# Batch 0's heads 0 to 3 loaded and attended ahead of heads 4 to 7, in a retention layer fused with a feed-forward layer

## The chip, the cores and the metric

The kernel runs on one core of a Trainium2 chip. A core has TensorE (matrix products and transposes, results into PSUM), VectorE, ScalarE and GpSimd (elementwise work), and SyncE, whose queue issues nearly all transfers here. PSUM has eight banks that the kernel shares out by tags. The metric is device time of one execution in microseconds (us). The kernel before takes 296.96 us, the median of three runs (296.57 to 297.06).

## The reference

Eight batches, eight heads, 576 positions, 64 numbers per head. Scores are masked and damped by a power of the distance, not normalised, and the result goes through a layer with a swish of a learned slope.

```python
scores = scale * np.matmul(q, k.transpose(0, 1, 3, 2))
gamma = 1.0 - 2.0 ** (-5.0 - np.arange(H))
rel = pos[:, None] - pos[None, :]
Dmat = np.where(rel >= 0, gamma[:, None, None] ** rel[None], 0.0)
attn = np.matmul(scores * Dmat, v)                 # (8, 8, 576, 64)
x = attn.transpose(0, 2, 1, 3).reshape(4608, 512)
h = x @ w_in                                       # 512 -> 2048
out = (h / (1.0 + np.exp(-beta * h))) @ w_out      # 2048 -> 512
```

## The kernel before

A power of a distance splits into two factors: queries are multiplied by `gamma**pos` (`gq`, with the scale in it), and either keys or values by `gamma**-pos` (`gvh` for batch 0, `gv` later). What is left of the damping is a mask of ones and zeros. Because nothing is normalised, earlier positions can be gathered in a state, the sum of key times value: a block's output is its own masked scores times values ("O") plus its queries times the state of all blocks before it ("cross").

The first 512 positions of each batch are attended in blocks, and batches follow one another; the last 64 positions of all batches make one more block of work. For each batch the outputs are laid down turned (`xT`), and the feed-forward layer runs on them: the up-projection `ph` (16 groups `fo` of 128 columns, each four products over `ko`, the four groups of 128 rows of `w_in`), a Silu on ScalarE into `gT`, and the down-projection `po` (16 products for each of four row groups `ms`). `ko` 0 and 1 need heads 0 to 3 alone, `ko` 2 and 3 heads 4 to 7. All is cast to bf16 before TensorE uses it. The order of all instructions is written out by hand (`manual_schedule`): each engine has one queue that it works in program order, and waits on semaphores of the others. `merged` weaves the lists `streams` into the list `fill`: an entry `(x, f)` is emitted before the fill item with the next number.

The change is in the first stage, batch 0, which nothing precedes. Its 512 positions are cut into two spans of 256 (`s` = 0, 1), and its heads into two halves (`a` = 0 for heads 0 to 3, 1 for 4 to 7). The steps, as functions:

- `load_q` (L75) and `load_span` (L99): SyncE issues the loads of queries (a half, 512 KB) and of keys or values (`j` = 0, 1; a span and half, 256 KB).
- `pre_q` (L282): VectorE scales queries, two operations for each half. `t_q` (L348): TensorE turns them, eight transposes for a half, and one copy brings them into `qT`; ScalarE copies for half 0, VectorE for half 1.
- `pre_s` (L456): GpSimd casts or scales keys or values. Half 0 casts its keys and scales its values, half 1 scales its keys and casts its values.
- `s_T` (L469): four transposes of keys, and ScalarE's copy into `kT`. `s_sc` (L483): sixteen score products, and two masks on VectorE into `R`.
- `s_O` (L497): sixteen products of values and masked scores. `s_st` (L519): products for the state, up to three block borders in PSUM tiles `s_sts`. `s_keep` (L530): two copies of a state into its tile `sbds`, on the engines that are passed in. `s_cross` (L508): queries times the state. `s_x` (L515): the copy into `xT`.
- `keep_warm` (L246): a product of the identity with itself, 512 columns, whose result nobody reads. The text calls it a filler.
- `betas`, `betas_safe` (L251, L256): the slopes are turned, and three small GpSimd operations keep them from being zero.

These are called one after the other on lines 726 to 780, and then the feed-forward layer begins: `cast_w_in` (L209) casts pieces of `w_in`, which SyncE loads ahead of all else behind the spans, as 256 or 512 columns of two or four row groups (`pieces`, L193). `ups` (L661) is an up-projection of several `fo` in two steps, `u` = 0 for `ko` 0 and 1 and `u` = 1 for 2 and 3; `up` (L648) does all four. `rest` (L782) has what of the attention is not needed for the first step: the crosses and `xT` of half 1. `last_products` and `last_state` make the state of the whole batch, for the last 64 positions. `down` (L681) splits the products of batch 0 from `fo` 5 on into two of 256 columns. The casts of `w_out` follow its loads.

## Time and profile before

| | us |
|---|---|
| median of three runs | 296.96 |
| the profiled execution's own time | 297.28 |
| its span | 295.5 |
| TensorE busy | 287.1 (97%) |
| ScalarE, GpSimd, VectorE busy | 145.9, 111.1, 102.5 |
| 5.79 to 16.66, attention of batch 0: span, TensorE busy | 10.87, 10.35 |
| 16.66 to 31.64, up-projection of batch 0: span, TensorE busy | 14.98, 14.86 |

Each instruction has a start and a duration; products are pipelined, so that the distance between starts, not the duration, is what a product costs in a stream. "Idle before" an instruction is put down to what released it. The chain of waits goes back from the last instruction to what released it. The profiled execution is one run; its own time is 1.8 us above its span and 0.32 above the median. Landings of loads are read from the semaphores of the transfers: low queries 4.93, high queries 6.42, keys and values from 7.32 to 13.61, pieces of `w_in` from 14.37 to 26.20.

### The profile page before, as it was taken

The numbers are of one execution on the slowest core, as the hardware profiler recorded it, in microseconds if no ns is written. First come the engines' busy times: TensorE is split into PE (matmuls) and PEld (weight loads), VectorE is DVE, ScalarE is ACT, GpSimd is POOL, SyncE is SP. The second block draws the span as 40 slices with busy tenths as digits, with TensorE's granted clock in tenths as the row PEclk, the third lists the DMA queues.
The fourth block names the chain that finished last, engine by engine and source line by source line (L and its number), as shares of the span: only waits on it lengthen the run. The fifth ranks groups of instructions, "written<-read, shape, count | busy, mean of one in ns | idle before, by whom it ended". The sixth has DMA issues, their size and how long they took to land.

```text
span 295.5 us, 7656 instructions
## 1 busy us (share of the span) xinstructions
PE 287.1 (97%) x3245; PEld 150.6 (51%) x3274; DVE 102.5 (35%) x213; ACT 145.9 (49%) x255; POOL 111.1 (38%) x219
## 2 busy tenths in 40 slices
PE   7999999999999999999999999999999999999995
PEld 3654587855544554445444544454554544444443
DVE  5764546604640551045204530354053500110012
ACT  5657537783278434843474347434780167007600
POOL 5957027955733713280438316754223000000000
PEclk9999999999999999999999999999999999999999
DMA  7999999999999898949999849998998110131011
GB/s 225 306 367 386 376 226 277 220 180 253 222 229 235 214 162 231 252 72 161 231 250 198 180 105 273 190 177 180 219 174 138 73 38 0 35 71 38 0 71 71
DMA packets 124033, 53.97 MB, mean 183 GB/s; under 512 B 101840, under 2 KB 116448, under 8 KB 124000
## 3 DMA queue, kind: packets, MB, share of 16 engines
q1 hardware_dynamic: 123968, 53.49, 82.1%
q8 instruction: 25, 0.41, 0.6%
q14 instruction: 8, 0.07, 0.1%
q10 hardware_dynamic: 32, 0.01, 0.0%
HBM read 36.71 MB, written 9.44 MB: 156 GB/s over the span
## 4 chain that ended last, share of the span: by engine, by line
PE 96%; DMA 1%; issue 1%; ACT 0%; DVE 0%; DVEq 0%
PE po L690 42%; PE ph L655 38%; PE ph L670 4%; PE O L614 2%; PE sc L568 1%; PE st L586 1%; DMA qn<-in_q_dram 1%; PE O L627 1%; PE T L352 1%; PE st L527 1%; PE sc L378 0%; PE sc L490 0%; PE O L504 0%; ACT kT L475 0%; PE ph L248 0%
## 5 line engine op out<-in xcount | busy, mean ns | idle before, releaser
L690 PE MATMUL po<-w_out_sb,gT 128*128 128x512 bf16 (+3 forms) x619 | 125.7, 358 | 2.3 <-issue 2.1
L657 ACT ACTIVATE gT<-ph,beta_sb 128x512 bf16<-128x512 f32 (+1 forms) x140 | 91.5, 659 | 50.9 <-PE ph L655 50.5
L655 PE MATMUL ph<-xT,w_in_sb 128*128 128x512 bf16 (+1 forms) x550 | 114.4, 364 | 0.5
L690 PEld LDWEIGHTS <-gT 128*128 128x128 bf16 x636 | 60.2, 98 | 60.7
L655 PEld LDWEIGHTS <-w_in_sb 128*128 128x128 bf16 x560 | 54.3, 98 | 57.5 <-DVE first L594 0.4
L697 DVE COPY ot<-po 128x512 f32<-128x512 f32 (+2 forms) x33 | 22.2, 672 | 72.2 <-PE po L690 69.4
L328 POOL CAST kn<-kvn 128x128 bf16<-128x128 f32 (+2 forms) x76 | 23.4, 343 | 46.1 <-DMA kvn<-in_k_dram 41.2
L295 POOL TENSOR_TENSOR qs<-qn,gq 128x256 bf16<-128x256 f32 (+1 forms) x36 | 26.3, 756 | 33.1 <-DMA qn<-in_q_dram 33.1
L575 DVE TENSOR_TENSOR R<-sc,tri 128x512 bf16<-128x512 f32 x28 | 17.4, 684 | 60.0 <-PE sc L568 60.0
L306 POOL TENSOR_TENSOR vn<-kvn,gv 128x512 bf16<-128x512 f32 x28 | 29.1, 1040 | 7.4 <-DMA kvn<-in_v_dram 7.1
L642 ACT CAST xT<-O 128x512 bf16<-128x512 f32 x14 | 7.5, 590 | 31.6 <-PE O L627 31.6
L597 ACT CAST sbd<-warm 128x256 bf16<-128x256 f32 x18 | 7.3, 407 | 25.6 <-DVE warm L594 20.6
L670 PE MATMUL ph<-xT,w_in_sb 128*128 128x512 bf16 x54 | 12.8, 379 | 0.1
L594 DVE TENSOR_TENSOR first<-st,warm 128x256 f32<-128x256 f32 x24 | 10.2, 425 | 2.9 <-ACT sbq L597 0.5
L316 POOL TENSOR_TENSOR kn<-tln,gq 128x128 bf16<-128x128 f32 (+1 forms) x12 | 5.6, 470 | 14.2 <-DMA tln<-in_q_dram 9.9
L594 DVE TENSOR_TENSOR warm<-st,first 128x256 f32<-128x256 f32 x18 | 7.6, 423 | 9.6 <-PE st L586 8.4
L673 ACT ACTIVATE gT<-ph,beta_sb 128x512 bf16<-128x512 f32 x14 | 8.7, 688 | 4.4 <-PE ph L670 4.4
L642 DVE CAST xT<-O 128x512 bf16<-128x512 f32 x14 | 9.0, 686 | 5.1 <-PE O L627 5.1
L214 POOL CAST w_in_sb<-wt 128x256 bf16<-128x256 f32 (+1 forms) x15 | 7.7, 530 | 5.0 <-DMA wt<-in_moe_w_in_dram 4.9
L597 ACT CAST sbd<-first 128x256 bf16<-128x256 f32 x18 | 7.3, 407 | 2.2 <-DVE first L594 0.2
L670 PEld LDWEIGHTS <-w_in_sb 128*128 128x128 bf16 x56 | 5.2, 97 | 6.3 <-issue 0.5
L231 DVE TENSOR_SCALAR w_out_sb<-wt,rbeta_sb 128x512 bf16<-128x512 f32 x13 | 5.9, 485 | 5.0 <-DMA wt<-in_moe_w_out_dram 5.0
(107 smaller groups left out, 166.1 us busy)
## 6 DMA issues: line engine op xcount, KB each, us to landing
qn<-in_q_dram SPq DMA_DIRECT2D x16, 512.0 KB, 5.2
kvn<-in_k_dram SPq DMA_DIRECT2D x32, 256.0 KB, 6.1
kvn<-in_v_dram SPq DMA_DIRECT2D x32, 256.0 KB, 5.1
out_dram<-ot SPq DMA_DIRECT2D x31, 256.0 KB, 3.4
wt<-in_moe_w_out_dram SPq DMA_DIRECT2D x8, 512.0 KB, 8.5
wt<-in_moe_w_in_dram SPq DMA_DIRECT2D x5, 512.0 KB, 8.8
wt<-in_moe_w_in_dram SPq DMA_DIRECT2D x6, 256.0 KB, 5.6
tln<-in_q_dram SPq DMA_DIRECT2D x8, 128.0 KB, 3.6
```

The costliest lines, as they stand in the source:

```text
L295: nc.gpsimd.tensor_tensor(batch[b]["qs"][:, cs, to], q_tiles[b][:, hs, cs].rearrange("p h i d -> p i h d"), gq[:, cs, hs].unsqueeze(3).to_ ...
L306: nc.gpsimd.tensor_tensor(live[i]["vn"], kv_tiles.pop(i)[:, 1], gains(gv, c), ALU.mult)
L328: nc.gpsimd.tensor_copy(kn[:, c % 2, to], t[:, 0, hs])
L575: nc.vector.tensor_tensor(R[x][:, j].rearrange("k c p q -> k (c p) q"), sc[x, j].rearrange("k c p q -> k (c p) q"), mask, ALU.mult)
L594: nc.vector.tensor_tensor(new[:], add, sums[(c - 1) % 2][:], ALU.add)
L597: nc.scalar.copy((sbq[c] if c < NC - 1 else ends[u])[:], new[:])
L642: (nc.scalar.copy if n % 2 else nc.vector.tensor_copy)(x, o)
L655: nc.tensor.matmul(ph, w_in_sb[:, ko, fo * P:(fo + 1) * P], xts[m][:, ko, :, w], start=(ko == 0), stop=(ko == KO - 1))
L657: nc.scalar.activation(gts[m][:, fo, :, w], ph, ACT.Silu, scale=beta_sb[:, fo:fo + 1])
L670: nc.tensor.matmul(phs[f][:], w_in_sb[:, ko, f * P:(f + 1) * P], xts[m][:, ko], start=(ko == 0), stop=(ko == KO - 1))
L690: nc.tensor.matmul(po[:, x:y], gT[:, fo, ms, :], w_out_sb[:, fo, n0 + x:n0 + y], start=(fo == 0), stop=(fo == FO - 1), skip_group_check=m ...
L697: (nc.scalar.copy if m == 0 else nc.vector.tensor_copy)(ot, po[:, :nn])
```

## The change

The loads of batch 0 come in another order: queries of heads 0 to 3, their keys, queries of heads 4 to 7, keys of span 0, values of heads 0 to 3, keys of span 1, values of heads 4 to 7. All keys are now cast and all values scaled. The turned queries of heads 4 to 7 are copied by ScalarE instead of VectorE in batch 0; two of the four copies of turned keys go to VectorE (`s_T` gets the engine and the bank passed in). The calls in the prelude are put in another order, with nine fillers in place of five, and `betas_safe` behind the first two key casts. The states are numbered by block, use other PSUM tiles, and the second span's are copied by ScalarE (two) and VectorE (one). `w_in`'s fourth piece is loaded in two transfers; `fo` 4 to 7 go through `ups`, the banks of the up-projection's results change, the last state products come one fill item earlier, and down-projections of batch 0 are split from `fo` 7 on.

```diff
--- before.py
+++ after.py
@@ -122,10 +122,11 @@
             for x in range(2):
                 nc.sync.dma_start(to[x * TL:(x + 1) * TL], src[2 * t + x, :, MB:, :].rearrange("h s d -> s h d"))
 
-    load_q(0)
-    span_order = [(s, j, a) for j in range(2) for a in range(2) for s in range(2)]
-    for x in span_order:
+    load_q(0, (0,))
+    for n, x in enumerate([(0, 0, 0), (1, 0, 0), (0, 0, 1), (0, 1, 0), (1, 1, 0), (1, 0, 1), (0, 1, 1), (1, 1, 1)]):
         load_span(*x)
+        if n == 1:
+            load_q(0, (1,))
     beta_rows = consts.tile([FO, P], F32, name="beta_rows")
     nc.scalar.dma_start(beta_rows[:], moe_beta.rearrange("(fo p) -> fo p", p=P))
 
@@ -190,7 +191,7 @@
     WG = 4
 
     low_rows, high_rows = slice(0, KO // 2), slice(KO // 2, KO)
-    pieces = [(f, 256, (low_rows, high_rows) if f < 768 else (slice(0, KO),)) for f in range(0, d_ff // 2, 256)]
+    pieces = [(f, 256, (low_rows, high_rows)) for f in range(0, d_ff // 2, 256)]
     pieces += [(f, 512, (w,)) for f in range(d_ff // 2, d_ff, 512) for w in (low_rows, high_rows)]
     NP = len(pieces)
     w_in_r = moe_w_in.rearrange("(ko ki) f -> ki ko f", ki=P)
@@ -243,10 +244,11 @@
             nc.tensor.matmul(ph[:, :cols], warm[:, :P], src, start=True, stop=True,
                              skip_group_check=True)
 
-    def keep_warm(tag="mm"):
+    def keep_warm(n=1, tag="mm"):
         ph = psum.tile([P, CB, P], F32, name="ph", tag=tag, bufs=3 if tag == "mm" else 1)
-        nc.tensor.matmul(ph[:], ident[:], ident[:].unsqueeze(1).to_broadcast([P, CB, P]), start=True, stop=True,
-                         skip_group_check=True)
+        for _ in range(n):
+            nc.tensor.matmul(ph[:], ident[:], ident[:].unsqueeze(1).to_broadcast([P, CB, P]), start=True, stop=True,
+                             skip_group_check=True)
 
     def betas():
         pb = psum.tile([P, FO], F32, name="pb", tag="mm", bufs=3)
@@ -350,7 +352,7 @@
         for i in range(CB):
             for p in range(2):
                 nc.tensor.transpose(T[:, i, p, :], heads(batch[b]["qs"][:, i], 2 * u + p), ident[:])
-        (nc.vector.tensor_copy if u else nc.scalar.copy)(batch[b]["qT"][:, :, 2 * u:2 * u + 2], T[:])
+        (nc.vector.tensor_copy if b and u else nc.scalar.copy)(batch[b]["qT"][:, :, 2 * u:2 * u + 2], T[:])
 
     def t_k(i):
         T = psum.tile([P, HP, P], BF16, name="T", tag="sc" if i in (CB + 2, CB + 3) else "O", bufs=2)
@@ -461,18 +463,18 @@
                             kT=sb.tile([P, 2, HP, P], BF16, name="kT", tag="kT", bufs=4),
                             vn=sb.tile([P, 2, H, D], BF16, name="vn", tag="vn", bufs=VB), R={})
         to, src = spans[s]["kv"[j] + "n"][:, :, w], span_tiles[s, j][:, w].rearrange("p h i d -> p i h d")
-        if a == j:
+        if j == 0:
             nc.gpsimd.tensor_copy(to, src)
         else:
             nc.gpsimd.tensor_tensor(to, src, gvh[:, 2 * s:2 * s + 2, w].unsqueeze(3).to_broadcast([P, 2, HP, D]), ALU.mult)
 
-    def s_T(s, a):
+    def s_T(s, a, tag, e):
         S = spans[s]
-        T = psum.tile([P, 2, 2, P], BF16, name="T", tag="O", bufs=2)
+        T = psum.tile([P, 2, 2, P], BF16, name="T", tag=tag, bufs=3 if tag == "mm" else 2)
         for i in range(2):
             for pl in range(2):
                 nc.tensor.transpose(T[:, i, pl, :], heads(S["kn"][:, i], 2 * a + pl), ident[:])
-        act(S["kT"][:, :, 2 * a:2 * a + 2], T[:])
+        e(S["kT"][:, :, 2 * a:2 * a + 2], T[:])
 
     def s_q(c, r, p):
         return batch[0]["qT"][r, :, p, c * PC:(c + 1) * PC]
@@ -519,7 +521,7 @@
     def s_st(a, n, s, rows, at=None, fresh=False):
 
         if n not in s_sts:
-            s_sts[n] = psum.tile([P, HP, P], F32, name="st", tag="mm" if n else "st", bufs=3 if n else 1)
+            s_sts[n] = psum.tile([P, 2 if n == 3 else HP, P], F32, name="st", tag="st" if n == 1 else "mm", bufs=1 if n == 1 else 3)
             fresh = True
         S, at = spans[s], 2 * a if at is None else at
         for i in range(2):
@@ -527,13 +529,13 @@
                 nc.tensor.matmul(s_sts[n][:, at + p, :], heads(S["kn"][rows, i], 2 * a + p), heads(S["vn"][rows, i], 2 * a + p),
                                  start=fresh and i == 0 and p == 0, stop=True, skip_group_check=True)
 
-    def s_keep(a, n, es, bank=None, at=None):
+    def s_keep(a, c, es, n=None, at=None):
 
         ps, at = slice(2 * a, 2 * a + 2), 2 * a if at is None else at
         for j in range(2):
-            st = s_sts[min(n, 1) if bank is None else bank][half(j), at:at + 2, half(j)]
-            if n < 3:
-                es[j](sbds[n][half(j), ps, half(j)], st)
+            st = s_sts[n or c][half(j), at:at + 2, half(j)]
+            if c < CB:
+                es[j](sbds[c - 1][half(j), ps, half(j)], st)
             else:
                 es[j](ends[0][half(1 - j if a else j), ps], st)
 
@@ -685,7 +687,7 @@
             pos_[ms] = psum.tile([P, d_model], F32, name="po", tag="mm" if m or ms < 3 else "st", bufs=3 if m or ms < 3 else 1)
         po = pos_[ms]
         for fo in range(f0, f0 + fn):
-            parts = ((0, nn),) if m or fo < 5 else ((0, nn // 2), (nn // 2, nn))
+            parts = ((0, nn),) if m or fo < 7 else ((0, nn // 2), (nn // 2, nn))
             for x, y in parts:
                 nc.tensor.matmul(po[:, x:y], gT[:, fo, ms, :], w_out_sb[:, fo, n0 + x:n0 + y],
                                  start=(fo == 0), stop=(fo == FO - 1), skip_group_check=m == 0)
@@ -725,55 +727,55 @@
 
     warm_up(2, MB)
     betas()
-    betas_safe()
     pre_q(0, 0)
     pre_q(0, 1)
     t_q(0, 0)
+    pre_s(0, 0, 0)
+    pre_s(1, 0, 0)
+    betas_safe()
+    keep_warm()
+    s_T(0, 0, "O", dve)
+    keep_warm(2)
+    s_T(1, 0, "O", act)
     pre_q(0, 2)
     pre_q(0, 3)
     keep_warm()
+    s_sc(0, 0, "sc")
+    s_sc(1, 0, "mm")
+    keep_warm(2, "st")
     t_q(0, 1)
-    keep_warm()
-    pre_s(0, 0, 0)
-    s_T(0, 0)
-    pre_s(1, 0, 0)
-    keep_warm()
-    s_sc(0, 0, "sc")
-    s_T(1, 0)
     pre_s(0, 0, 1)
+    s_T(0, 1, "O", act)
+    pre_s(0, 1, 0)
+    keep_warm(3, "st")
+    pre_s(1, 1, 0)
     pre_s(1, 0, 1)
-    keep_warm()
-    s_T(0, 1)
-    s_sc(1, 0, "mm")
-    pre_s(0, 1, 0)
-    pre_s(1, 1, 0)
-    keep_warm("st")
-    s_T(1, 1)
+    s_st(0, 2, 0, whole_span)
+    s_st(0, 3, 0, whole_span, 0)
+    s_st(0, 1, 0, low)
+    s_keep(0, 2, (act, act))
+    s_keep(0, 1, (act, act))
     s_sc(0, 1, "sc")
+    s_O(0, 0, "O")
+    s_st(0, 3, 1, low, 0)
+    s_keep(0, 3, (act, act), 3, 0)
+    s_T(1, 1, "mm", dve)
+    s_O(1, 0, "O")
     pre_s(0, 1, 1)
     pre_s(1, 1, 1)
-    s_st(0, 1, 0, whole_span)
-    s_keep(0, 1, (act, act))
-    s_st(0, 0, 0, low)
-    s_keep(0, 0, (act, act))
-    s_O(0, 0, "O")
+    for c in range(1, CB):
+        s_cross(c, 0)
+    s_x(0, 0, act)
+    s_x(0, 1, act)
     s_sc(1, 1, "mm")
-    s_st(0, 1, 1, low)
-    s_keep(0, 2, (act, act))
-    s_O(1, 0, "O")
-    s_cross(1, 0)
-    s_cross(2, 0)
-    s_x(0, 0, act)
-    s_cross(3, 0)
-    s_x(0, 1, act)
-    s_st(1, 1, 0, whole_span)
-    s_st(1, 0, 0, whole_span, 0, True)
-    s_st(1, 0, 0, low)
-    s_st(1, 0, 1, low, 0)
-    s_keep(1, 1, (dve, dve))
-    s_keep(1, 0, (dve, dve))
-    s_keep(1, 2, (act, act), 0, 0)
     s_O(0, 1, "sc")
+    s_st(1, 2, 0, whole_span)
+    s_st(1, 1, 0, whole_span, 0, True)
+    s_st(1, 1, 0, low)
+    s_st(1, 1, 1, low, 0)
+    s_keep(1, 2, (act, act))
+    s_keep(1, 1, (act, act))
+    s_keep(1, 3, (dve, dve), 1, 0)
     s_O(1, 1, "sc")
     cast_w_in(0, (0, 1), (1,))
     cast_w_in(1, (0, 1), (1,))
@@ -788,17 +790,16 @@
         nc.vector.reciprocal(rbeta_sb[:], beta_sb[:])
 
     def last_products():
-        s_st(0, 1, 1, high)
-        s_st(1, 1, 1, whole_span)
+        for a in range(2):
+            s_st(a, 2, 1, whole_span)
 
     def last_state():
         for a in range(2):
-            s_keep(a, 3, (dve, dve))
-
-    fill = [F(ups, 0, (fo, fo + 1), u, tags) for u in range(2) for fo, tags in ((0, ("mm", "mm")), (2, ("O", "O")))]
-    fill += [F(ups, 0, (4, 5), u, ("sc", "sc")) for u in range(2)]
-    fill += [F(up, 0, fo) for fo in (6, 7)]
-    for fo, tags in ((8, ("O", "O", "sc", "sc")), (12, ("mm", "mm", "mm", "st"))):
+            s_keep(a, CB, (dve, dve), 2)
+
+    fill = [F(ups, 0, (fo, fo + 1), u, tags) for u in range(2) for fo, tags in ((0, ("O", "O")), (2, ("mm", "mm")))]
+    fill += [F(ups, 0, (fo, fo + 1), u, (tag, tag)) for fo, tag in ((4, "sc"), (6, "O")) for u in range(2)]
+    for fo, tags in ((8, ("mm", "mm", "sc", "sc")), (12, ("O", "O", "mm", "st"))):
         for u in range(2):
             fill += [F(ups, 0, range(fo, fo + 4), u, tags), lambda: None]
     d0 = len(fill)
@@ -839,7 +840,7 @@
                 nc.gpsimd.affine_select(out=t[w], in_=t[w], pattern=pattern, compare_op=ALU.is_ge,
                                         fill=0.0, base=0, channel_multiplier=-1)
 
-    streams = [[(d0 + 2, F(triangles)), (1, rest), (2.5, F(last_products)), (3.6, F(last_state))], [(0, F(load_w_out, 0)), (1.6, F(cast_w_in, 2)), (2.1, F(cast_w_in, 3)), (2.2, F(load_w_out, 1)),
+    streams = [[(d0 + 2, F(triangles)), (1, rest), (1.9, F(last_products)), (3.6, F(last_state))], [(0, F(load_w_out, 0)), (1.6, F(cast_w_in, 2)), (2.1, F(cast_w_in, 3)), (2.2, F(load_w_out, 1)),
                 (4.1, F(cast_w_in, 4)), (6.1, F(cast_w_in, 5)), (6.2, F(load_w_out, 2)), (8.1, F(cast_w_in, 6)),
                 (10.1, F(cast_w_in, 7)), (10.2, F(load_w_out, 3))],
                [(d0 - 4 + 3.3 * g, F(cast_w_out, g)) for g in range(WG)],
```

## What was predicted

> **What bounds the kernel now.** I read the page from the top, then the chain of waits and the order of time of each engine over the first 32 us, because the edits end there: behind the first 38 us every queue holds the same instructions in the same order in both kernels.
>
> ```profile
> PE 287.1 (97%) x3245; PEld 150.6 (51%) x3274; DVE 102.5 (35%) x213; ACT 145.9 (49%) x255; POOL 111.1 (38%) x219
> PEclk9999999999999999999999999999999999999999
> PE 96%; DMA 1%; issue 1%; ACT 0%; DVE 0%; DVEq 0%
> ```
>
> TensorE is the bound, and from 12.1 us on it has next to no gap: a microsecond won or lost before the first up-projection (L670) moves the end by as much, unless it is lost again to an input that comes late. So the question is when L670 starts (16.66) and what lies between it and the first down-projection (31.64). The chain of waits over that stretch:
>
> ```profile
> 7.03 0.43 PE ph L248
> 8.43 0.43 PE ph L248
> 9.32 0.59 ACT kT L475
> 10.74 0.59 ACT kT L475
> 12.35 0.35 PE sc L490 x16
> 16.15 0.57 PE O L504 x32
> 19.93 0.66 PE st L527 x8
> 20.58 2.59 PE ph L670 x12
> ```
>
> Twice TensorE waits for ScalarE's copy of turned keys. A filler (L248) of 512 columns takes 0.43 at 8.43, while twelve products of as many columns take 2.59 at 20.58, 0.216 each. In order of time:
>
> ```profile
> 5.79 1.25 PE L352 MATMUL T<-ident,qs 128*128 128x128 bf16 x8 [0.54 <-DVE qs L298]
> 9.08 0.63 PE L248 MATMUL ph<-ident 128*128 128x512 bf16 x1
> 9.96 0.42 PE L490 MATMUL sc<-qT,kT 64*64 64x128 bf16 x16 [0.25 <-ACT kT L475]
> 10.54 0.38 PE L248 MATMUL ph<-ident 128*128 128x512 bf16 x1
> 7.38 1.51 POOL L465 CAST kn<-kvn 128x512 bf16<-128x512 f32 x2 [0.16 <-DMA kvn<-in_k_dram]
> 9.20 2.04 POOL L467 TENSOR_TENSOR kn<-kvn,gvh 128x512 bf16<-128x512 f32 x2 [0.31 <-DMA kvn<-in_k_dram]
> 11.20 2.04 POOL L467 TENSOR_TENSOR vn<-kvn,gvh 128x512 bf16<-128x512 f32 x2
> 13.18 1.17 POOL L465 CAST vn<-kvn 128x512 bf16<-128x512 f32 x2
> 14.42 2.66 POOL L214 CAST w_in_sb<-wt 128x256 bf16<-128x256 f32 x7
> 8.47 0.69 DVE L353 COPY qT<-T 128x1024 bf16<-128x1024 bf16 x1 [0.70 <-PE T L352]
> 10.49 5.03 DVE L493 TENSOR_TENSOR R<-sc,causal 128x512 bf16<-128x512 f32 x8 [1.33 <-PE sc L490]
> ```
>
> One filler lasts 0.63 at 9.08 and 0.38 at 10.54: between these TensorE's rate doubles, though the granted clock reads 9 throughout. I put the step at 9.8.
>
> **The change, part by part.** Call heads 0 to 3 "low", 4 to 7 "high", the two 256-position spans 0 and 1. "Walk" means that I went down the queues in program order with the durations of these rows; for the kernel before it gives 16.68 for the first L670, against 16.66.
>
> *Loads.* By their landings, 512 KB of queries take 1.49 us and a span part 0.90. Low queries land at 4.93 in both. Before, high queries land at 6.42 and the keys at 7.32, 8.22 (low), 9.12, 10.03 (high). After: low keys 5.83 and 6.73, high queries 8.22, high keys of span 0 9.12, low values 10.03 and 10.93, then the last high keys 11.84 and high values as before by 13.61. The bytes ahead of w_in are the same, so w_in lands as before. One load of w_in becomes two issues of 0.37 to 0.47 on SyncE, which has issued all eleven by 16.3, while the last of them lands at 26.2: nothing.
>
> *GpSimd.* All keys become casts (0.61), all values multiplications (1.04): 4 x 1.04 + 4 x 0.61 as before. The three small beta operations (L258 to 260, 1.6 with their gaps) move behind two casts that wait for loads; they fill 7.4 to 9.0, before the next landing at 9.12. Their reader, the first Silu at 19.81, does not notice. By landing or by queue the last value is ready at 14.8 instead of 14.35, and the casts of w_in follow 0.4 later. First to need them is L670, after 17.0 in my walk; two casts are done by 15.6.
>
> *Low half.* First turn of queries 5.79 as before, a slow filler, then turned keys of span 0 at 7.25 (before: 8.65). VectorE copies them, 0.425 by the copy of the same shape on line 359, to 8.35. The next turn, of span 1, waits for that copy (bank "O"); two slow fillers, 7.68 to 8.53, fill the wait, so they cost about 0.1. ScalarE's copy ends at 9.79, covering the next filler; scores of span 1 start at 9.84 instead of 11.38. These are 1.5 us won, but on the low heads alone.
>
> *High half.* Two fillers at full rate (0.43) stand ahead of the turn of high queries, whose scaling (2 x 0.61 from 8.28) is long done: uncovered. Turn 10.65 to 11.1; copied by ScalarE, 1.01 from 11.3, where VectorE took 0.69. Behind it on ScalarE waits the copy of high keys, +0.91, done at 12.8. The three fillers at 11.3 lie under that. Scores of span 0, high: 12.85, before 12.28. From here a chain through VectorE: two masks (0.60 each) from 13.3, the copy of the last keys behind them (0.43) to 14.9, scores 14.98, two masks from 15.44 to 16.7, value products 16.78, L670 at 17.10. TensorE has its state products and low outputs in between and stands only 0.3 in all. The three fillers' end and ScalarE's copy meet within 0.05: neither alone could be taken away.
>
> Sum to here: 17.10 - 16.66 = +0.44.
>
> *Between up- and down-projection.* Before, the last state products (eight, four of them with 64 rows) start at 19.86, and 0.656 passes from the slot behind the product before them to the next L670: two changes of tile shape at 0.095 and 8 x 0.056. After, all eight have 128 rows: 8 x 0.056 = 0.45, so -0.21. They also move one step earlier, ahead of the products that waited 0.17 for VectorE's xT (18.51 to 18.90): the same 0.45 now covers that, -0.17. The four state products more in the prelude are in the walk. Down-projections of fo 5 and 6 lose their split: eight pairs of 0.219 become eight of 0.216, -0.03. The products' new banks are all free in time in the walk. The state copies that go from VectorE to ScalarE (0.27 each there, 0.30 here) end at 17.3 with four, and with two more on VectorE at 17.9; the cross products that read them stand behind four up-projections, at 18.0 and 18.2: covered.
>
> Inputs further on: the tightest w_in cast of before ends 1.3 us ahead of its product (19.10 to 20.42), batch 1's scaled queries and cast keys 1.9 (41.43 to 43.40, 41.90 to 43.84), so up to 1.3 us of gain would pass through, and a loss passes whole.
>
> Sum: 0.44 - 0.21 - 0.17 - 0.03 = **+0.03**. The profiled execution took 297.28 (span 295.5 and 1.8 around it), so 297.31; the median, 0.32 below it, becomes **297.0**.
>
> Bounds. The step of the rate is not set by anything in the program. With it at 6.4 the walk gives 16.36, at 8.0 16.67, at 11.0 17.70, at 12.0 18.15: the sum then runs from -0.71 to +1.08. I take 9.8, the time of this trace, since TensorE's start at 5.79 and its filling since are the same. Hops between engines: 0.04 to 0.06 where one condition is waited for, but 0.116 for the mask that waited for two (10.378 to 10.494) and 0.146 for the product that waited for three. With 0.08 more on each hop the high chain ends 0.69 later. I take the short ones, which most waits here are.
>
> [...]
>
> **Rivals.**
> 1. *Slower: the hops of the high chain.* Place: query turn, ScalarE, scores, two masks, key copy, scores, two masks, values. At 0.08 more a hop: +0.03 + 0.69, 297.7; it decides from 0.07 on. For it: TensorE has only 0.3 to give. Against: the hops of the low keys ran at the short price (turned 9.28, copied from 9.32; copied 9.91, scores 9.96).
> 2. *Faster: an earlier step.* From 5.79 to 9.5 fillers stream for 1.28 us before and 1.71 after. A step at 7.0 gives -0.65, at 6.4 -0.71: 296.3. It decides (over 0.6) from about 7.2 down. Against: the fillers at 8.22 and 9.08 were slow still, behind a stretch in which TensorE had hardly stood.
> 3. *Slower: a later step*, at 11.5 to 12: by the walk +0.78 to +1.08, 297.9; it decides from 11.0 on. Against: TensorE idles less before 9.8 than it did.
>
> **How the numbers follow.** 0.2% is 0.6 us, about what a measurement of this kernel can tell from no change. Forecast 0.50 (its own range 296.6 to 297.4), rival 1 0.18, rival 2 0.22, rival 3 0.10. Faster 0.22, same 0.50, slower 0.28. The range 296.2 to 297.9 reaches into all three and leaves out under 2 in 10.
>
> **What would show it.** Right: scores of span 1, low, near 9.8; scores of span 0, high, near 12.85; first up-projection near 17.1, first down-projection within 0.3 of 31.64; no gap between the last state products and the up-projection after them; the beta operations between 7.4 and 9.1. Wrong: a short filler before 9 us (rival 2), or a long one after 10.5 (rival 3); VectorE's second pair of high masks starting after 15.9 (rival 1); up-projections that wait for w_in casts.

## The result, and the profile after

The changed kernel takes 297.85 us (median of 20 runs, 297.06 to 299.09), the kernel before, run beside it, 296.94 (20 runs, 296.50 to 298.21). The ratio is 1.0029, with a 95% interval of 1.0016 to 1.0042: the change makes the kernel slower by some 0.9 us. Ratios here leave disturbed runs out and medians do not, so a ratio can differ a little from the quotient of two medians.

The first profile does not show this loss. Its execution took 297.19 us, the second lowest of the 20, and the profiled execution of before 297.28, above its median. So the changed kernel was profiled once more, and that execution took 298.18. The table sets the three side by side. "Step" is the time at which TensorE's rate doubles, taken from the trace's record of the clock (in the second profile, with the step at 9.37, two fillers of 512 columns take 0.85 at 8.19 and three take 0.65 at 11.77, 0.43 and 0.22 each); "rest" is what follows the first down-projection.

| us | before | after, first profile | after, second profile |
|---|---|---|---|
| profiled execution | 297.28 | 297.19 | 298.18 |
| step of the rate | 10.00 | 5.68 | 9.37 |
| low queries landed | 4.93 | 4.81 | 5.28 |
| high queries landed | 6.42 | 8.61 | 9.34 |
| last values landed | 13.61 | 13.98 | 14.60 |
| first turn of queries | 5.79 | 5.66 | 6.13 |
| first up-projection | 16.66 | 16.70 | 17.46 |
| first down-projection | 31.64 | 31.76 | 32.51 |
| between the two | 14.99 | 15.06 | 15.05 |
| rest | 263.9 | 263.7 | 264.0 |

From the page of the changed kernel (first profile), the busy times, the granted clock in 40 slices, and the chain by engine:

```profile
PE 286.7 (97%) x3245; PEld 149.6 (51%) x3274; DVE 102.0 (35%) x212; ACT 145.8 (49%) x256; POOL 111.1 (38%) x219
PEclk9999999999999999999999999999999999999999
PE 92%; DMA 2%; SPq 2%; POOL 1%; issue 1%; DVE 0%
```

TensorE still bounds the kernel, with the same number of products. The chain is new in one place: it now leaves TensorE early on. The changed kernel's chain of waits, first profile, in order of time (start, length, what):

```profile
7.09 6.02 DMA kvn<-in_v_dram
13.11 0.07 issue
13.18 2.04 POOL vn L469 x2
15.23 2.08 POOL w_in_sb L215 x6
17.31 0.05 issue
17.36 0.38 PE ph L672
...
18.29 0.28 issue
18.57 0.82 PE ph L672 x3
19.39 0.45 PE st L529 x8
```

Two things are to be seen. The values, which land late, and GpSimd's casts of `w_in` behind them lead up to the up-projection at 17.36. And at 18.29 there is "issue": TensorE stands for 0.28, and the profile shows nothing that it waits for. The next weight load starts 0.71 behind the one before it (17.85, 18.56). TensorE's instructions in order of time show the same gap in the line of 18.57, and a filler that lasts 0.38 at 6.49, where fillers of before lasted 0.63 until 9.08:

```profile
5.66 0.40 PE L354 MATMUL T<-ident,qs 128*128 128x128 bf16 x4 [0.41 <-DVE qs L300]
...
6.49 0.38 PE L250 MATMUL ph<-ident 128*128 128x512 bf16 x1
...
16.70 1.04 PE L672 MATMUL ph<-xT,w_in_sb 128*128 128x512 bf16 x3
17.91 0.38 PE L672 MATMUL ph<-xT,w_in_sb 128*128 128x512 bf16 x1
18.57 0.82 PE L672 MATMUL ph<-xT,w_in_sb 128*128 128x512 bf16 x3 [0.28 <-issue]
```

So the equal spans of the two first profiles (295.5) compare a step at 5.68 with one at 10.00. The second profile of the changed kernel, with its step at 9.37, is the one to set against before. Its chain of waits:

```profile
6.13 1.21 PE T L354 x8
...
10.14 0.42 PE sc L492 x16
...
13.24 0.35 PE sc L492 x16
...
15.31 0.42 PE sc L492 x16
...
17.53 0.54 PE ph L672 x2
...
18.50 0.34 PE O L514 x6
18.83 0.22 PE ph L672
19.05 0.27 issue
19.32 0.82 PE ph L672 x3
20.14 0.45 PE st L529 x8
```

It starts 0.34 later than before did, at the first turn (the low queries landed 0.35 later, at 5.28), and has the same "issue", now at 19.05. Against the profile of before the first up-projection comes 0.80 later, the stretch to the down-projection is 0.06 longer, and the rest 0.06: 0.92, of which the profiled times show 0.90.

### The profile page after: what moved, and what is told of

It is laid out like the page before. It is cut to its first block, busy times and chain, and to the rows that moved or that the text cites. A ratio compares the mean times of both kernels' runs of the same rounds, so it can differ in the third digit from the quotient of the medians.

```text
span 295.5 us, 7656 instructions
## 1 busy us (share of the span) xinstructions
PE 286.7 (97%) x3245; PEld 149.6 (51%) x3274; DVE 102.0 (35%) x212; ACT 145.8 (49%) x256; POOL 111.1 (38%) x219
## 4 chain that ended last, share of the span: by engine, by line
PE 92%; DMA 2%; SPq 2%; POOL 1%; issue 1%; DVE 0%
PE po L692 42%; PE ph L657 37%; PE ph L672 5%; DMA kvn<-in_v_dram 2%; SPq L104 2%; PE O L616 2%; PE st L588 1%; PE sc L570 1%; PE O L629 1%; POOL w_in_sb L215 1%; POOL vn L469 1%; PE sc L380 0%; PE O L416 0%; PE st L439 0%; SPq L84 0%
## 5 line engine op out<-in xcount | busy, mean ns | idle before, releaser
L659 ACT ACTIVATE gT<-ph,beta_sb 128x512 bf16<-128x512 f32 (+1 forms) x138 | 89.8, 657 | 50.9 <-PE ph L657 50.6
L657 PE MATMUL ph<-xT,w_in_sb 128*128 128x512 bf16 (+1 forms) x542 | 112.5, 363 | 0.5
L692 PEld LDWEIGHTS <-gT 128*128 128x128 bf16 x628 | 59.5, 98 | 61.4
L672 PE MATMUL ph<-xT,w_in_sb 128*128 128x512 bf16 x62 | 14.4, 379 | 0.4 <-issue 0.3
L675 ACT ACTIVATE gT<-ph,beta_sb 128x512 bf16<-128x512 f32 x16 | 9.8, 687 | 4.7 <-PE ph L672 2.6
L672 PEld LDWEIGHTS <-w_in_sb 128*128 128x128 bf16 x64 | 6.1, 98 | 7.4 <-issue 0.6
```

The source lines that it names most:

```text
L657: nc.tensor.matmul(ph, w_in_sb[:, ko, fo * P:(fo + 1) * P], xts[m][:, ko, :, w], start=(ko == 0), stop=(ko == KO - 1))
L659: nc.scalar.activation(gts[m][:, fo, :, w], ph, ACT.Silu, scale=beta_sb[:, fo:fo + 1])
L672: nc.tensor.matmul(phs[f][:], w_in_sb[:, ko, f * P:(f + 1) * P], xts[m][:, ko], start=(ko == 0), stop=(ko == KO - 1))
L692: nc.tensor.matmul(po[:, x:y], gT[:, fo, ms, :], w_out_sb[:, fo, n0 + x:n0 + y], start=(fo == 0), stop=(fo == FO - 1), skip_group_check=m ...
```

## The experiments

Theory 1 was that the order itself loses in the first 32 us, even where the rate steps up at the same time; theory 2, its rival, that the difference lies in when the rate steps up. Theory 3 came with the second group of runs: the nine fillers hold the rate, and pay for that with their time. Each group had the kernel before run beside it on the same chip: 297.31 for the first four kernels, 297.46 for the next four, 297.52 for the last.

### An early step in both orders

Between the turned slopes and the first turn of queries TensorE idles for 0.41 to 0.88 us. Two fillers there, in the order of before and in the changed one:

```diff
     betas()
+    keep_warm()
+    keep_warm()
     betas_safe()
...
     betas()
+    keep_warm(2)
     pre_q(0, 0)
```

> Kernel before, with two fillers more in TensorE's idle time between the turned slopes and the first turned queries (5.25 to 5.79). Theory 1 (when TensorE's rate doubles is a matter of each execution, 10.0 in the profile of before and 5.7 in that of after, and at an equal step the new order itself loses 0.7 to 0.9): the gap closed, the step comes by 8 us in every execution, the spread of the times shrinks, and the median falls by 0.3 to 0.5 against before. Theory 2 (the new order makes the step come later, and loses by that alone): also a fall here, but then the partner kernel with the new order falls to the same time. If the step has nothing to do with how TensorE is filled before 5.8: no change, within 0.2.

> Changed kernel, with the same two fillers at the same place. Theory 1: falls by 0.2 to 0.5 as well, so it stays 0.7 to 0.9 above the kernel before with these fillers, and ends 0.3 to 0.6 above the kernel before. Theory 2: ends within 0.3 of the kernel before with these fillers.

Before's order: 296.97 (296.70 to 297.63), ratio 0.9993 [0.9985, 1.0002], step at 5.06 instead of 10.00. The spread of its 12 runs is 0.93, where 29 runs of before beside it spread over 2.34. Most of that difference is not the step: six of the 29 have a mean granted clock of 0.989 to 0.994, none of the 12 is below 0.998, and the other 23 spread over 1.12. The changed order: 297.79 (296.88 to 298.84), ratio 1.0020 [1.0006, 1.0033], step at 5.88. With the step early in both, the changed order is 0.82 slower by the medians and 0.69 by the profiled runs (297.39, 296.70). Of these 0.69, 0.39 stand at the first up-projection (16.59, 16.20), 0.17 in the stretch behind it (15.15, 14.98) and 0.18 in the rest, less 0.05 by which the parts around the spans differ. The first turn was itself 0.51 later (6.14, 5.63), behind low queries that landed at 5.29 and 4.78. Theory 1 holds, theory 2 falls: an early step in both does not take the loss out of the changed order.

What the fillers do to the step needs a closer reading. In all 14 profiles the stretches that the record of the clock gives between its changes are whole multiples of 3.413 us (286.72 at the full rate in before and 290.13 in the first profile of the changed kernel are 84 and 85 of them), and where their borders lie differs between executions: the two profiles of the changed kernel have one at 5.68 and one at 5.96. TensorE was busy for 0.88 to 1.00 of the 3.41 us ahead of the first step in all 14. In the four profiles with a late step the 3.41 us ahead of those hold all or most of the idle gap, and TensorE was busy for only 0.79 to 0.83 of them (before, 3.17 to 6.59: 2.85 us). Of the nine profiles with the two fillers, four have the step (4.35 to 5.06) ahead of the first filler (4.85 to 5.15), and three (5.20 to 5.42) at most 0.24 behind its start. Only in the changed order here (step at 5.88) and in one later kernel (6.66) did the 3.41 us hold the whole gap, filled. That the fillers bring the step forward rests on these two; in the others the step may have come early without them.

### Two single suspects of the changed order

First the scores of span 0's high heads ahead of the state products that wait for scaled values:

```diff
+    s_sc(0, 1, "sc")
     s_st(0, 2, 0, whole_span)
...
     s_keep(0, 1, (act, act))
-    s_sc(0, 1, "sc")
```

> Changed kernel, with the scores of span 0, heads 4 to 7, ahead of the first three groups of state products (which wait for scaled values until 11.5) and of their copies, instead of behind them. In the profile of after these scores had their keys at 11.9 and started at 12.41. If the values that GpSimd scales late hold the chain of the high heads, scores start near 12.0, masks near 12.4, and the up-projection 0.3 to 0.45 earlier: 0.3 under the changed kernel. If the chain is held elsewhere (key copies, or the weight casts behind the values on GpSimd): within 0.1 of the changed kernel, about 0.9 above before.

298.53 (298.10 to 299.15), ratio 1.0042 [1.0027, 1.0057]: worse. TensorE's instructions of this kernel in order of time:

```profile
11.72 0.81 PE L250 MATMUL ph<-ident 128*128 128x512 bf16 x3
13.25 0.42 PE L492 MATMUL sc<-qT,kT 64*64 64x128 bf16 x16 [0.72 <-ACT kT L477]
13.60 0.95 PE L529 MATMUL st<-vn,kn 128*128 128x128 bf16 x12
```

The scores wait for ScalarE's copy of the keys, and the state products that had covered it wait behind them. I had taken that wait of scores for values for a loss; it was cover.

Then the two fillers that stand ahead of the turn of high queries, the ones that the prediction called uncovered:

```diff
     s_sc(1, 0, "mm")
-    keep_warm(2, "st")
     t_q(0, 1)
```

> Changed kernel without the two fillers between the low scores and the turn of the high queries. The prediction had them uncovered, 0.43 of TensorE's time: then 0.3 to 0.4 under the changed kernel. In the profile of after the turn's second half waits for scaled queries until 9.98 anyway: then nothing in executions with an early step, 0.2 or less in the median.

297.85 (297.11 to 300.08), ratio 1.0021 [1.0003, 1.0040]: no gain shows, though the interval would still hold one of 0.3. The two slowest runs (298.98, 300.08) have a mean granted clock of 0.994. In the second profile of the changed kernel the high keys are cast until 11.12 and TensorE turns them at 11.38; without the fillers it would stand there. In this run's own profile the cast was done by 10.35 and the keys were turned at 10.89 without a wait, and TensorE stood for 0.19 later on, ahead of the state products at 12.34, where the chain leads back to VectorE's masks. The step came at 10.12, and the stretch between up- and down-projection was 14.61, near the length that the prediction forecast (14.58) and that the first profile did not have.

### Without the nine fillers, and with five of them

The changed order with the two early fillers, and without any of the nine:

```diff
     betas_safe()
-    keep_warm()
     s_T(0, 0, "O", dve)
-    keep_warm(2)
     s_T(1, 0, "O", act)
...
     pre_q(0, 3)
-    keep_warm()
     s_sc(0, 0, "sc")
     s_sc(1, 0, "mm")
-    keep_warm(2, "st")
...
     pre_s(0, 1, 0)
-    keep_warm(3, "st")
```

> Changed kernel with the two fillers before 5.8, but without its nine fillers. In the profiles of after and of its twin with two more fillers, TensorE stands 0.44 to 0.48 at its 223rd weight load for no semaphore, 2.5 us after a 16 KB packet of instructions started on a transfer engine; the kernel before is past 19.8 when it comes to its 223rd. Theory 1 (TensorE runs ahead of its instructions): with nine pairs fewer ahead, the 223rd falls nine pairs later in the program, the stall goes, the stretch from first up- to first down-projection falls from 15.1 to 14.6 to 14.7, and the time by 0.3 to 0.6 against the twin with fillers, unless the fillers held TensorE's rate. Theory 2 (the stall belongs to the product, L672, or to its bank): it stays at the same product and the time falls by 0.1 or less. Theory 3 (fillers hold the rate): the rate falls back or steps late, products of 512 columns last 0.63 after 6 us, and the time rises by 0.5 or more.

299.21 (296.54 to 300.54), ratio 1.0037 [1.0004, 1.0070], in two groups: four runs at 296.54 to 296.81, eight at 298.62 to 300.54. The profile is of the second group (300.39). Busy times of the engines by stretch (stretch, its length, busy us and instructions of PE, PEld, DVE, ACT and POOL, granted clock, DMA share, GB/s):

```profile
5.20:12.00 6.80, 4.06 (x63) 2.31 (x63) 4.22 (x8) 2.71 (x5) 3.84 (x7) 1.00 1.08 296
12.00:18.90 6.90, 6.68 (x114) 5.15 (x113) 3.79 (x7) 3.34 (x11) 6.57 (x13) 0.51 1.06 327
```

TensorE was busy for 4.06 of 6.80, and then the granted clock fell to one half, from 12.03 to 18.86. The first up-projection starts at 19.89. In the 3.41 us ahead of the fall TensorE was busy for 1.61. So in this order the nine fillers held the rate (with them, in the first run of the changed order with the early fillers, none of the 12 mean granted clocks is below 0.998): theory 3. The two groups bear it out: the four low runs have a mean granted clock of 0.999 or 1.000, the eight others 0.983 to 0.993. So where the rate holds, the same order costs some 296.7, though no such run was profiled.

With five of the nine:

```diff
     betas_safe()
-    keep_warm()
     s_T(0, 0, "O", dve)
-    keep_warm(2)
+    keep_warm()
...
-    keep_warm(2, "st")
+    keep_warm(1, "st")
...
-    keep_warm(3, "st")
+    keep_warm(2, "st")
```

> The changed order with the two fillers after the turned slopes and five of its nine fillers instead of all or none. Fillers hold the rate (theory 3): with none of the nine the times fell into two groups, four at 296.54 to 296.81 and eight at 298.6 to 300.5; with five, most executions should hold the rate and the order then loses its walk through the four others: median 296.7 to 297.3. If the rate needs all of them, two groups again, median above 298. If fillers cost nothing and hold nothing, 297.8 as with nine.

297.17 (296.68 to 298.77), ratio 0.9990 [0.9970, 1.0009], seven of ten runs at or below 297.44. In the profile TensorE was busy for 6.00 of the 7.60 us from 4.40 to 12.00 and the rate held. Nine fillers seem more than this needs: of the three runs at 298.0 and above one (298.77) has a mean granted clock of 0.994, and the other two have 1.000, so that their loss is of another kind, which stays open. Against the nine (1.0020 [1.0006, 1.0033]) the intervals overlap a little. The stall is there, too, but short (0.15).

### Both halves of the queries first

The changed order with the two early fillers, but the high queries loaded right behind the low ones, as before:

```diff
-    load_q(0, (0,))
+    load_q(0)
...
         load_span(*x)
-        if n == 1:
-            load_q(0, (1,))
```

> Changed kernel with the two fillers before 5.8, and both halves of the queries loaded first, the spans behind them in the changed order. In four profiles of the changed order the high queries, loaded between spans, begin with packets of up to 0.77 us and land 0.25 to 0.7 later than the bytes allow, and all behind them with them (last values 13.9 to 14.3, where the kernel before has 13.5 to 13.6). Theory: the going back to the queries costs it; then the last values land at 13.4 to 13.6 here and no packet at the start of the high queries is over 0.25, while low keys land 1.5 later; the high half gains 0.3 and the low half no longer leads, so that the time falls by 0.1 to 0.4 against the twin. If the loads are as late here: the lag is not of the order, and the time is the twin's or up to 0.5 longer.

298.38 (298.18 to 299.62), ratio 1.0036 [1.0021, 1.0051]. I had expected 0.1 to 0.4 less than with the high queries in between (297.79), and it is not faster. So the loads can be on time and the order still lose. The last values land at 13.38. In the six profiles that load all queries first they land at 13.38 to 14.02, mean 13.63; in the eight that come back to the queries between spans at 13.83 to 14.60, mean 14.18. In seven of those eight the longest 1 KB packet between 4.5 and 7.5 us took 0.44 to 0.77 us, in the other 0.23; in the six, 0.06 to 0.13. But half of the difference is there before the orders part: the low queries, first in both, land at 4.68 to 5.05, mean 4.84, in the six, and at 4.81 to 5.29, mean 5.11, in the eight. Only 0.28 of the 0.55 arise behind them, and what delays the low queries is not known. With all queries first the low keys land at 7.11 and 7.99 instead of 5.70 and 6.78, TensorE idles for 0.99 of the two microseconds from 7 to 9, and then works almost without a gap to the first up-projection at 17.16. The stall is there as well:

```profile
18.03 0.44 PE L512 MATMUL O<-qT,sbd 128*128 128x128 bf16 x5
19.03 0.23 PE L512 MATMUL O<-qT,sbd 128*128 128x128 bf16 x1 [0.56 <-issue]
```

### What the stall is

Counted from the start, the weight load at which TensorE stands has the same number in each of the five profiles of the changed order that show the stall, whatever it is: the pair of weight load and product with the number 223, counted from zero, called the 223rd here. That is an up-projection (L672) in the changed kernel, a low cross product (L514 there, L512 here) in two others. The trace also records one 16 KB packet of instructions in this stage, on a queue of its own. It takes 1.1 to 1.2, and in none of the profiles of the table does the 223rd pair start less than 2.41 us after it does; what passes in the 1.3 to 1.5 between its end and the pair behind a stall the trace does not tell:

| kernel | packet starts | 222nd pair | 223rd pair | after the packet |
|---|---|---|---|---|
| after, first profile | 16.11 | 17.85 | 18.56 | 2.46 |
| after, second profile | 16.91 | 18.62 | 19.31 | 2.41 |
| changed order, early fillers | 15.71 | 17.63 | 18.27 | 2.55 |
| the same, all queries first | 16.37 | 18.20 | 19.03 | 2.65 |
| before | 16.12 | 19.86 | 19.87 | 3.75 |
| before, early fillers | 15.22 | 18.66 | 18.88 | 3.65 |

The kernel before has eight pairs fewer ahead of its first up-projection (204, against 212), gets to the 223rd 3.65 to 3.75 after the packet, and does not wait. Of the changed order, the kernel with the moved scores and the one without the two fillers ahead of the high queries' turn reach it after 2.63 and 2.42 and show no such stop either. To test the count, fillers of 512 columns were each cut into four of 128, which makes three more pairs for the same columns. In before's order, with the early fillers, this was done to the other five fillers (15 pairs more):

```diff
+    def keep_quarters(n=1, tag="mm"):
+        ph = psum.tile([P, CB, P], F32, name="ph", tag=tag, bufs=3 if tag == "mm" else 1)
+        for x in range(4 * n):
+            nc.tensor.matmul(ph[:, x % CB], ident[:], ident[:], start=True, stop=True, skip_group_check=True)
...
     pre_q(0, 3)
-    keep_warm()
+    keep_quarters()
```

> The order of the kernel before, with the two fillers after the turned slopes, and from its five other fillers each 512-column product cut into four of 128 columns: the same columns, 15 more pairs of weight load and product ahead of the first up-projection, nothing else. Supply of instructions (my theory of the 0.4 to 0.8 us in which TensorE stood for no semaphore): the stall belongs to the 223rd pair and to a 16 KB instruction packet that is done about 2.45 us after it starts. Here the 223rd pair lies 15 pairs earlier, beside the first up-projections, near 16.4 us, ahead of the packet's arrival near 17.7: TensorE stands there for 0.5 to 1.3 us though this order showed no such stall, part of it comes back from the 0.57 us wait for the turned outputs just behind, and the first down-projection comes 0.3 to 0.7 later than 31.18: 297.3 to 297.7. Rival (the stall is of the changed order's own instructions, a bank or a copy that comes late): no stall, 296.97 within 0.2.

297.78 (297.54 to 299.56), ratio 1.0015 [1.0001, 1.0029], against 0.9993 without the cut. The profiled run is 0.84 above that of the uncut one (297.54, 296.70). The chain of waits of the uncut kernel, then of the cut one:

```profile
16.27 0.97 PE ph L670 x4
17.23 0.34 PE O L512 x6
17.57 0.86 PE ph L670 x4
...
18.44 1.02 PE ph L670 x4
```

```profile
16.21 0.54 PE ph L675 x2
16.75 0.73 issue
17.48 0.38 PE ph L675
...
18.19 0.86 PE ph L675 x4
...
19.07 1.02 PE ph L675 x4
```

Up to 16.2 the cut kernel is as early as the other (first up-projection 16.14 and 16.20); then TensorE stands for 0.73 in the middle of an up-projection, at the 223rd pair (17.25, after 16.16), 2.64 after the start of its packet (14.61). The stretch to the first down-projection is 15.67 instead of 14.98. With 15 pairs more the order of before stands for 0.73, at the same count as the changed order: that much is shown.

The same in the changed order, on its five fillers in the tag "st":

```diff
-    keep_warm(2, "st")
+    keep_quarters(2, "st")
...
-    keep_warm(3, "st")
+    keep_quarters(3, "st")
```

> The changed order with the two fillers after the turned slopes, and the five fillers in the tag st cut into four products of 128 columns each: 15 more pairs, the same columns. Supply of instructions: the stall moves with the count, to the 223rd pair, which is now among the value products of the last scores ahead of the first up-projection (near 16.3 us instead of 17.63), and grows, since the packet comes no earlier: the first up-projection starts 0.5 to 1.5 later than 16.59, the stretch to the first down-projection falls from 15.15 to about 14.6, and the time is 297.9 to 298.8 against 297.79. Rival (an instruction's own dependency): the stall stays among the low cross products or the up-projection behind them, 297.79 within 0.3.

297.83 (296.96 to 298.41), ratio 1.0000 [0.9988, 1.0012], and my expectation fell in part. The packet started earlier too, at 13.87 instead of 15.71, and the 223rd pair, now among the last value products, came at 16.98, 3.11 after it, without a stall. TensorE's instructions in order of time:

```profile
17.24 1.04 PE L677 MATMUL ph<-xT,w_in_sb 128*128 128x512 bf16 x3
18.11 0.50 PE L519 MATMUL O<-qT,sbd 128*128 128x128 bf16 x6
18.45 1.03 PE L677 MATMUL ph<-xT,w_in_sb 128*128 128x512 bf16 x4
19.31 0.61 PE L534 MATMUL st<-vn,kn 128*128 128x128 bf16 x8
```

No gap: the stretch is 14.61, as forecast, here with an early step (5.42). The first up-projection is late (17.24) because the loads were: high queries at 9.11, last values at 14.44. Whether the changed order without its stall stands level with before is not shown: the ratios (1.0000 against 1.0020) say so, but their intervals overlap, the median did not fall (297.83, 297.79), and the loads were later. What starts the packet stays open: it started 1.5 to 3.9 us after the 96th pair, and with no count of pairs at a fixed distance.

In before and in the changed kernel the trace has 25 such packets of 16 KB and 6,519 recorded weight loads and products, an estimated 261 to a packet (the one count by the other); whose instructions a packet holds it does not tell. At this one count TensorE stood for 0.15 to 0.73 us in six profiles. That it waits there for instructions of the packet is my reading of the times, not shown.

### The changed kernel once more

> The changed kernel as it is, one more profile: its first profile was its second fastest execution. Theory 1 (the order itself loses in the first 32 us, by late landings and the stall for instructions): any further execution differs from 297.19 by what the first down-projection comes later than 31.76, within 0.15, and the rest behind it takes 263.7 to 264.0. Rival (the loss lies in the stages behind 38 us): the rest takes over 264.3 and the first down-projection is within 0.15 of 31.76.

The profile is the second one above: down-projection 0.75 later than in the first, rest 0.23 more and 264.0. That is more than the 0.15 that theory 1 allowed behind the first down-projection, so it holds in the main only: three quarters of the difference between the two executions (0.99) arose ahead of 32 us, and against before 0.86 of 0.92.

### What of the change is worth taking

Two of its edits were put into before's order with early fillers: the last state products one fill item earlier, and the split of down-projections from `fo` 7 on. In the second kernel the filler in the tag "st" at 11.7 was dropped as well:

```diff
-            parts = ((0, nn),) if m or fo < 5 else ((0, nn // 2), (nn // 2, nn))
+            parts = ((0, nn),) if m or fo < 7 else ((0, nn // 2), (nn // 2, nn))
...
-(2.5, F(last_products))
+(1.9, F(last_products))
...
-    keep_warm("st")
```

> Kernel before with the two fillers before 5.8, its last state products one fill item earlier (ahead of the up-projections that wait for VectorE's xT) and down-projections split from fo 7 on instead of 5: parts of the change done alone. By the prediction's terms -0.17 and -0.03, so 0.2 under the kernel before with these fillers, and 14.8 from first up- to first down-projection instead of 14.98. If the wait is not VectorE's but one for instructions, which come at a fixed time, the products pass into it: within 0.1.

> The same, and without the filler ahead of the turn of the second span's high keys, which the kernel before runs at 11.73 with no wait behind it: 0.22 less again (0.4 under the kernel before with fillers, 0.6 to 0.7 under before). If ScalarE's key copies hold the prelude there: within 0.1 of the former.

297.21 (296.47 to 297.85), ratio 0.9989 [0.9975, 1.0004]; and without the filler **296.80** (296.44 to 297.43), ratio 0.9981 [0.9968, 0.9994], lower than both kernels of this case, and its interval lies below that of no change. Against before's order with the early fillers alone (0.9993 [0.9985, 1.0002]) both intervals overlap, so the 0.2 and 0.4 that I expected of these edits cannot be told from nothing by the times. The chain of waits of the first:

```profile
16.78 0.97 PE ph L670 x4
...
18.08 0.86 PE ph L670 x4
18.95 0.66 PE st L527 x8
19.60 3.45 PE ph L670 x16
```

The state products (L527) now stand where the wait for VectorE's `xT` was, and the stretch is 14.81, 0.17 less than 14.98.

## Why the prediction was right or wrong

Forecast was no change, 297.0 with a likely range of 296.6 to 297.4; measured 297.85, inside the whole range (296.2 to 297.9) by 0.05 and outside the likely one. That it lies inside is luck: the upper end was drawn for longer hops and a later step. The case that came, slower by over 0.2%, had a chance of 0.28, but not for the reason that made it slower. The sum was +0.03; the second profile, whose step (9.37) is near the one assumed (9.8), gives +0.92. Step by step:

- **What bounds it.** Right. TensorE is the bound, and what is lost ahead of 32 us stays lost: the rest is 263.7 to 264.0 in all three profiles.
- **Loads.** Wrong, and the first term that failed. "High queries 8.22, high keys of span 0 9.12, by 13.61" became 8.61, 9.50, 13.98 and 9.34, 10.24, 14.60. Low queries, whose place did not change, landed at 5.28 instead of 4.93 in the second profile, though at 4.81 in the first. I had moved landings about as blocks of a fixed length, with equal bytes ahead of the last. Coming back to the queries went with last landings 0.55 later on average (eight profiles against six), of which 0.27 stands already at the low queries; why was not settled.
- **GpSimd.** The beta operations lie at 7.4 to 8.3 and 8.4 to 9.3, about where they were forecast, and took 0.9, not 1.6. But the cast of span 0's high keys took 0.83 and 0.82, not 0.61 (the row of before that I had read shows two casts in 1.51, so one had taken longer there, too), and the casts of `w_in` start at 15.17 and 15.85 instead of 14.42: 0.75 and 1.43 later, not 0.4. In the first profile they have no cover left, and TensorE waits 0.05 for one at 17.31.
- **Low half.** Right. In the second profile keys turned at 7.55, copy done at 8.65, scores of span 1 at 10.14: each 0.30 behind the walk (7.25, 8.35, 9.84), which is the late start.
- **High half.** The walk held, the start did not. High scores came at 13.17 (12.85 forecast), masks at 13.63 (13.3), second scores at 15.31 (14.98), second masks at 15.77 (15.44), first up-projection at 17.46 (17.10). The difference is 0.32 to 0.36 all along, and the first turn was already 0.34 late. With the early step of the first profile it is the same size: the walk gave 16.36 for a step at 6.4, measured 16.70. That the two fillers are "uncovered" is not borne out: without them no gain showed, and TensorE stood for 0.19 later on.
- **Between up- and down-projection.** The mechanism and the sum were right, and the gain was eaten (one price was loose: two changes of shape at 0.095 and eight products at 0.056 make 0.64, not 0.656). The earlier place gives 0.17 (14.98 to 14.81, in before's order); all that was forecast gives 14.61, 0.38 less than 14.99, in the four profiles without the stall. But the changed kernel itself had 15.06 and 15.05. The term that I did not have is a stall of 0.44 to 0.45 at the 223rd pair; that the instructions come too late there is my reading, not shown. In the five profiles with a stall whose packet times stand above, the 222nd pair started 1.55 to 1.92 us after the packet, and in the two of before's order in the table, which have none, 3.44 and 3.74; the new order is through the first 222 pairs 1.2 to 2.0 sooner than before's (17.85 and 18.62, against 19.86).
- **The rate.** I wrote that nothing in the program sets the step. That is half wrong. Where the borders of the 3.41 us stretches lie differs between executions of one program: the changed kernel had its step at 5.68 in one profile and at 9.37 in the other. But how busy a stretch is, is the program's doing: the idle gap ahead of the first turn left the stretches up to 5.96, 6.59, 6.70 and 7.10 busy for 0.79 to 0.83, and the step came one stretch later. In the run without the nine fillers step, fall and second step (5.20, 12.03, 18.86) lie 6.83 us apart, twice 3.41. A plain threshold does not come out of these traces: in that run the 3.41 us up to 15.44 were busy for 0.94, and the rate came back only at 18.86.
- **The rivals.** The hops of rival 1 stayed short (second high masks 15.77, below the 15.9 that I named). Rival 2, the early step, did come in the first profile and gave no gain: late loads and the stall took it. Rival 3 was not seen. The one that came, an engine that stands for no semaphore, was not on my list.

The miss adds up: +0.36 at the first up-projection, +0.47 in the stretch (14.58 by the sum of its terms, 15.05 measured), +0.06 in the rest, together 0.89. The stall is shown by experiment. The first term is not: 0.34 of it is the late first turn, behind low queries that landed late, and whether the new order of loads does that or chance is open.

## What to carry to other kernels

Before you compare two profiles, look at what differs between executions of one kernel, above all the time of the rate's step (5.68 and 9.37 here); two equal spans (295.5) hid most of a microsecond (the medians are 0.91 apart). Count TensorE's instructions as well as their time: in five profiles of the changed order TensorE stood at one count, the 223rd pair, for 0.15 to 0.56 us, and "issue" in the chain, with no releaser, is the line that tells it. In four of 14 profiles a stretch of 3.41 us with an idle gap, busy for 0.79 to 0.83, went by without the step, which came one stretch later, so fill such a gap where it is cheap. Count on a load's landing only within the spread that several profiles show (last values: 13.38 to 14.60).

## What the runs showed of the hardware

- TensorE stood for 0.15 to 0.73 us, in six of 14 profiles, at a fixed count of instructions (the 223rd pair); in the five of them whose packet times stand above it went on 2.41 to 2.65 us after a 16 KB packet of instructions had started, and the packet itself took 1.1 to 1.2.
- The first doubling of TensorE's rate came at 4.35 to 6.66 us in ten profiles and at 9.37 to 10.52 in four. The 3.41 us ahead of it were busy for 0.88 or more; in the four, the 3.41 us before those had an idle gap, were busy for 0.79 to 0.83 and were not followed by the step. In the run without the nine fillers, behind 3.41 us with 1.61 of work, the granted clock fell to 0.5 for 6.83 us, with no single gap over 0.84.
- A mean granted clock of 0.994 in a run's record is what 3.41 us at half the rate make of a run of 297 us (an estimate, half of 3.41 by 297). The profiled run with 6.83 at the half rate (300.39 us) has 0.989. By that estimate the rate fell back in eight of the twelve runs without the nine fillers (0.983 to 0.993).
- GpSimd's cast of 128x512 took 0.82 to 0.91 in the two profiles of the changed kernel where VectorE scaled queries beside it, and 0.61 or 0.62 where it did not. GpSimd's instructions of the changed kernel, second profile, in order of time:

```profile
6.22 0.91 POOL L467 CAST kn<-kvn 128x512 bf16<-128x512 f32 x1 [2.39 <-DMA kvn<-in_k_dram]
7.86 0.61 POOL L467 CAST kn<-kvn 128x512 bf16<-128x512 f32 x1 [0.72 <-DMA kvn<-in_k_dram]
...
10.30 0.82 POOL L467 CAST kn<-kvn 128x512 bf16<-128x512 f32 x1 [0.98 <-DMA kvn<-in_k_dram]
...
13.20 0.61 POOL L467 CAST kn<-kvn 128x512 bf16<-128x512 f32 x1
```

VectorE's scaling ran from 5.38 to 6.67 and from 9.36 to 10.65, beside the first and the third of these.
